# Second head of the first pair: hashed in 32x32 tiles, signs written in place, copies by ScalarE

## The chip, the cores and the metric

The kernel runs on one core of one Trainium2 chip. The metric is the time of one execution in device microseconds, as the median of several runs. A profiled execution gives the trace; its times are counted from the first instruction of the span.

## What is computed

Attention with a hash mask, then a mixture of small adapters. Four batches of eight heads, 768 positions, head size 64. The part that the change touches is the mask: a query and a key see each other only if the signs of their six projections agree.

```python
q_bits = (np.einsum('bhsd,dk->bhsk', q, proj) > 0)      # six bits a position
k_bits = (np.einsum('bhsd,dk->bhsk', k, proj) > 0)
...
mask = q_bucket[:, :, :, None] == k_bucket[:, :, None, :]
scores = scale * np.matmul(q, k.transpose(0, 1, 3, 2))
scores = np.where(mask, scores, -1000000000.0)
...
return np.matmul(attn, v).astype(np.float32)
```

Behind it, for each of the 3072 rows of the joined heads: the two best of eight experts by `x @ w_gate`, and their low-rank products added to `x`.

## The kernel before

The 32 heads are worked off as 16 pairs, `p` = 0 to 15. Each pair has six slots, `s` = 0 to 5. In a slot TensorE writes 128x1536 scores (`score`, L283), two blocks of 128 keys by 768 queries; slots 0 to 2 belong to the first head and 3 to 5 to the second. ScalarE takes the exponential of each (L286) into the tile `P`. Two PSUM buffers hold the scores, so the scores of a slot can be written while those of the slot before are being read. There are 96 slots. The order of everything is written out by hand: `slot` emits the scores and then the list `work(p)[s]`, and each engine runs its instructions in the order in which they are emitted.

The mask is worked into the score matmul. The operand tile `aug[p % 3]` has, for each of six blocks of 128 positions and for each of q and k of the two heads, 64 rows of the transposed head, six rows of signs (+0.5 or -0.5) and one row of a constant (1.0 for q, -1.5 for k). The contraction goes over these 71 rows; six equal signs add 1.5, which the constants take away, and any unequal sign leaves a negative number that the exponential, scaled by 128, sends to nothing.

How the rows get there, for pairs 1 to 15:

- `loadqk` (L152) and `loadv` (L160) fetch q, k and v from HBM on SyncE's queue, `natcast` (L232) makes bf16 of q and k on GpSimd, and `trq` (L241, TensorE) with `qcopy` (L247, VectorE), or a DMA transpose, puts them into `aug`. GpSimd's `shift` (L261) moves the second head's rows.
- `turn32` (L180) transposes 32x32 blocks of the same data on VectorE into `R`. `hash` (L193) multiplies `R` with the projection `hst` on TensorE, four groups of 32 output partitions (q and k of the two heads). `sign` (L205) compares with zero on VectorE into the tile `sg`.
- In `sg` the signs do not stand on the partitions where `aug` needs them. `signs_out` (L212) writes them to a DRAM tile `dr`, and `signs_in` (L220, or L224 for one head) reads them back into rows 64 to 71 of `aug`. The eight rows include the constant, which is made of `ssc`.

Pair 0 has a path of its own in `start`, because nothing else is there to hide its latencies. Its first head is transposed in fp32 by TensorE (`T1`, L540), copied out by ScalarE (`tcopy`, L544), cast into `aug` by ScalarE and GpSimd (`cast0`, L562), hashed from the transposed copy (`hash_here`, L568), and its signs are written straight into `aug` (`sign_here`, L575). Its second head is cast by GpSimd (`natcast0`, L548), transposed by TensorE (`tb0`, L553) and copied into `aug` by VectorE (`bcopy0`, L557), in slots 0 and 1; its signs take the way through `hash`, `sign` and DRAM, with `signs_out` on ScalarE's queue and `signs_in` on SyncE's queue in slot 0. `first(s)` emits what belongs to the first six slots. In `consts`, L90 writes the constant row of the first head with two memsets on VectorE.

The second product, of `P` with v, is `uni` (L291, one matmul that opens the sum) and `pvk` (L303, six matmuls for each block of keys), with `norm` (L321, L323) behind it. For pair 0 and its first head it stands in slots 4 and 5.

PSUM has two pools beside the two buffers of the scores: `m` with one buffer (hash, `trq`, router) and `vt` with one buffer (`tbB`, the transposes of pair 1's k, the sums of the second product).

Of the kernel before, what the change touches and what calls it, by code (L numbers as in the profile page):

```python
# [12 lines left out]
F32 = mybir.dt.float32  # L13
BF16 = mybir.dt.bfloat16
AX = mybir.AxisListType
ALU = mybir.AluOpType
# [3 lines left out]
class Emitter:  # L20
# [57 lines left out]
    def consts(self):  # L78
        nc, P, T, D, S = self.nc, self.P, self.T, self.D, self.S
        sg = self.singles  # L80
        self.wz = sg.tile([P, 512], BF16, name="wz")
        nc.vector.memset(self.wz, 0.0)
        self.dume = sg.tile([P, 1], F32, name="dume")
        nc.scalar.activation(out=self.dume, in_=self.wz[:, 0:1], func=ACT.Exp)
        self.ident = sg.tile([P, P], F32, name="ident")
        make_identity(nc, self.ident)
        self.aug = [sg.tile([P, T, 4, P], BF16, name=f"aug{i}") for i in range(3)]
        self.vb = [sg.tile([P, 2, T + 1, D + 1], BF16, name=f"vb{i}") for i in range(3)]
        for i in range(2):
            nc.vector.memset(self.aug[0][64:96, :, i, :], 1.0 if i == 0 else -1.5)  # L90
        self.eps = sg.tile([P, P], BF16, name="eps")
        nc.gpsimd.memset(self.eps, 2.0 ** -56)
        self.ident_bf = sg.tile([P, P], BF16, name="ident_bf")
        nc.gpsimd.tensor_copy(out=self.ident_bf, in_=self.ident)
        self.wa = sg.tile([P, self.nD, self.LZ], BF16, name="wa")
        self.Bcat = sg.tile([self.ER, self.Dm], BF16, name="Bcat")
        self.wg = sg.tile([P, self.nD, self.E], F32, name="wg")
        w = self.x3.tile([P, 2, self.Dm], F32, tag="acc", name="w")
        self.wA, self.wB = w[:, 0].rearrange("p (t z) -> p t z", t=self.nD), w[:, 1]
        for a in self.vb:  # L100
            nc.gpsimd.memset(a[:, :, 0:T, D:D + 1], 1.0)
            nc.gpsimd.memset(a[:, :, T:T + 1, D:D + 1], float(T))
        self.hst = sg.tile([P, 2, 8, 4], F32, name="hst")
        nc.gpsimd.memset(self.hst, 0.0)
        ssc = self.ssc = sg.tile([P, 1], F32, name="ssc")
        iq = sg.tile([P, 2], F32, name="iq")
        row = self.ident.rearrange("p (j b i) -> p j b i", j=4, b=8)
        nc.vector.memset(ssc, 0.5)
        for k in range(2):
            nc.vector.tensor_reduce(out=iq[:, k:k + 1], in_=row[:, k::2, 6, :], axis=AX.XY, op=ALU.add)  # L110
        for k, d in enumerate((-1.5, 1.0)):
            nc.vector.scalar_tensor_tensor(out=ssc, in0=iq[:, k:k + 1], scalar=d, in1=ssc,
                                           op0=ALU.mult, op1=ALU.add)
# [388 lines left out]
    def product(self, b, i, ps, start=True):  # L502
        self.nc.tensor.matmul(out=ps, lhsT=self.zT[b, i], rhs=self.Bcat, start=start, stop=True,  # L503
                              skip_group_check=not start)
# [38 lines left out]
    def tcopy(self, i):  # L543
        self.nc.scalar.mul(out=self.qkT[:, i, :], in_=self.tr["f", i][:, 0:384], mul=1.0 if i else 2.0 ** -10)  # L544

    def natcast0(self):
        for i in range(2):
            self.nc.gpsimd.tensor_copy(out=self.nb0[:, i], in_=self.nat[0][:, i, 1])  # L548

    def tb0(self, ps):  # L550
        for i in range(2):
            for u in range(3):
                self.nc.tensor.transpose(out=ps[:, i, u, :], in_=self.nb0[:, i, u * 128:(u + 1) * 128],  # L553
                                         identity=self.ident_bf)

    def bcopy0(self, e, ps):
        self.nc.vector.tensor_scalar(out=self.aug[0][0:64, e::2, 2:4, :].rearrange("p u i c -> p i u c"),  # L557
                                     in0=ps[64 * e:64 * e + 64], scalar1=2.0 ** -5, scalar2=None, op0=ALU.mult)

    def cast0(self, i, f):  # L560
        for e in range(2):
# [18 lines left out]
    def start(self):  # L580
        nc, P = self.nc, self.P
        sy, ac = nc.sync, nc.scalar
        self.proj3 = self.singles.tile([P, 32], F32, name="proj3")
        ac.dma_start(out=self.proj3[:, 0:6], in_=self.proj.unsqueeze(0).to_broadcast([2, 64, 6]))
        for h in range(2):
            for i in range(2):
                self.loadqk(0, i, h, sy)
        self.loadqk(1, 0, None, sy)
        self.loadqk(1, 1, None, sy)
        self.loadv(0, sy)  # L590
        self.loadqk(2, 0)
        self.loadqk(2, 1)
        nc.vector.memset(self.proj3[:, 6:32], 0.0)
        self.consts()
        self.qkT = self.singles.tile([P, 2, 384], F32, name="qkT")
        self.nb0 = self.singles.tile([P, 2, 384], BF16, name="nb0")
        w = [self.ps_s.tile([P, 3, 512], F32, tag="s", name="warm0")[:, 0], self.vt([P, 512], F32, "warm1")]
        warm = lambda n, i=1: self.warm(n, w[i])
        hq = self.ps_s.tile([P, 3, 512], F32, tag="s", name="hq")
        hk = self.ps_s.tile([P, 3, 512], F32, tag="s", name="hk")  # L600
        warm(5, 0)
        self.T1(0)
        self.T1(1, hk)
        warm(1)
        self.tcopy(0)
        self.tcopy(1)
        self.hst_fill(0, "dve")
        self.hst_fill(1, "pool")
        self.turn32(0, 0, 1)
        self.turn32(0, 1, 1)  # L610
        self.cast0(0, nc.scalar.copy)
        self.cast0(1, nc.gpsimd.tensor_copy)
        self.natcast0()
        self.hash_here(0, hq)
        self.hash_here(1, hk)
        self.hash(0, (1,))
        self.sign_here(0, hq, 0)
        self.sign_here(0, hq, 1)
        self.sign(0, (1,))
        self.signs_out(0, (1,), ac)  # L620
        for us in (slice(0, 1), slice(1, 3)):
            for e in range(2):
                self.sign_here(1, hk, e, us)

    def warm(self, n, w):
        for i in range(n):
            self.nc.tensor.matmul(out=w, lhsT=self.wz[:, 0:128], rhs=self.wz, start=True, stop=True)

    def first(self, s):
        if s == 0:  # L630
            tbB = self.tbB = self.vt([self.P, 2, 3, 128], BF16, "tbB")
            self.tb0(tbB)
            self.turn32(1, 0, 0)
            self.turn32(1, 1, 0)
            self.bcopy0(0, tbB)
            self.natcast(1, 0)
            self.natcast(1, 1)
            self.signs_in(0, (1,))
            self.loadv(1)
        if s == 1:  # L640
            self.hash(1, (0,))
            self.sign(1, (0,))
            self.signs_out(1, (0,))
            self.loadqk(3, 0)
            self.bcopy0(1, self.tbB)
            self.vcast(0)
        if s == 2:
            self.trq(1, 0)
            self.qcopy(1)
            self.trq(1, 1, self.vt)  # L650
            self.qcopy(1, 1)
            self.turn32(1, 0, 1)
            self.turn32(1, 1, 1)
            self.shift(1, 0)
            self.shift(1, 1)
            self.signs_in(1, (0,))
            self.loadqk(3, 1)
            self.natcast(2, 0)
            self.natcast(2, 1)
        if s == 3:  # L660
            self.hash(1, (1,))
            self.sign(1, (1,))
            self.signs_out(1, (1,))
            self.loadqk(4, 0)
            self.turn32(2, 0, 0)
            self.turn32(2, 0, 1)
            self.signs_in(1, (1,))
            self.vcast(1)
        if s == 4:
            self.turn32(2, 1, 0)  # L670
            self.turn32(2, 1, 1)
        if s == 5:
            self.trq(2)
            self.qcopy(2)
            self.shift(2, 0)
# [15 lines left out]
    def work(self, p):  # L691
# [3 lines left out]
        b, L, Ls, D = self.plan(p)  # L695
# [75 lines left out]
            add(4, "loadqk", n4, 1)  # L771

        if not last:
            kA = {4: (0, 1, 2), 5: (3, 4, 5)} if p == 0 else {4: (0, 1, 2, 3), 5: (4, 5)} if p == 1 or Ls == 3 else {
                3: (0, 1), 4: (2, 3), 5: (4, 5)}
            for s in sorted(kA):
                if s == min(kA):
                    add(s, "uni", p, 0)
                add(s, "pvk", p, 0, kA[s])
            add(5, "norm", p, 0)  # L780
# [7 lines left out]
        for s in sorted(D):  # L788
            d, i = D[s]
# [176 lines left out]
```

## Time and profile before

| | us |
|---|---|
| median of three runs | 167.91 |
| the three runs | 166.63, 167.91, 171.59 |
| the profiled execution | 167.42 |
| its span, first to last instruction | 165.6 |
| busy in the span: TensorE matmul | 149.5 |
| ScalarE | 143.6 |
| VectorE | 110.4 |
| GpSimd | 110.4 |

In the rows of the profile PE is TensorE, PEld its weight loads, DVE VectorE, ACT ScalarE, POOL GpSimd; SPq and ACTq are the queues of DMA issues of SyncE and ScalarE. A row of a timeline gives the start in us, the length in us, engine, line, instruction, output <- inputs, how many were merged, and in brackets the idle time before it with what ended it. A row of a group gives the busy time, the mean ns of one, and the idle time before. The ends of matmuls are modelled. One fp32 matmul appears as two records. The mean granted TensorE clock is 0.986.

### The profile page before, as it was taken

The page shows a single profiled execution, that of the slowest core. Times are in us where ns is not written, and L with a number is a line of the kernel's source. Part 1 is how long each engine was busy: PE and PEld are TensorE (multiplying, and loading weights), DVE is VectorE, ACT ScalarE, POOL GpSimd, SP SyncE. Part 2 cuts the span into 40 slices and gives each one's busy share as a digit, 9 for nine tenths or more (in the row PEclk, how much of TensorE's full clock was granted, in tenths as well). Part 3 has the DMA queues.
Part 4 walks back from the last instruction along what each step waited for, and adds up shares of the span by engine and source line. Part 5 has one row for each costly group of instructions (what it writes and reads, how often), then busy time and mean ns, then how long its engine had stood idle before and what let it go on. Part 6 is the DMA issues. An engine that isn't in the chain of part 4 may idle for free.

```text
span 165.6 us, 5300 instructions
## 1 busy us (share of the span) xinstructions
PE 149.5 (90%) x2148; PEld 101.8 (61%) x2148; DVE 110.4 (67%) x290; ACT 143.6 (87%) x122; POOL 110.4 (67%) x164
## 2 busy tenths in 40 slices
PE   6787998997999999999998999899999999999840
PEld 2244675675666666666765677576756666879500
DVE  5786895554747699486858696659766545656770
ACT  3466989798999999899998999989999999998640
POOL 3688969696878879694979397948976742510060
PEclk9999999999999999999999999999999999999995
DMA  5874659999999999999989999999998950439036
GB/s 146 279 246 117 199 125 205 260 237 224 169 202 190 211 190 241 185 214 340 256 178 254 321 255 155 251 247 285 174 245 153 248 94 4 86 124 294 6 132 248
DMA packets 58331, 33.09 MB, mean 200 GB/s; under 512 B 43714, under 2 KB 56002, under 8 KB 58306
## 3 DMA queue, kind: packets, MB, share of 16 engines
q1 hardware_dynamic: 57632, 32.46, 89.0%
q8 instruction: 17, 0.28, 0.7%
q10 hardware_dynamic: 674, 0.29, 0.6%
q14 instruction: 8, 0.07, 0.2%
HBM read 20.18 MB, written 7.05 MB: 164 GB/s over the span
## 4 chain that ended last, share of the span: by engine, by line
PE 49%; DMA 20%; DVE 16%; POOL 4%; issue 3%; SPq 3%; ACT 1%; DVEq 1%; POOLq 0%
PE s L283 21%; DMA nat<-in_k_dram 13%; PE pv L303 11%; DMA aug<-dr 5%; PE hs L193 4%; DVE R L180 3%; DVE acc L524 3%; PE pv L291 2%; DMA dr<-sg 2%; DVE x L323 2%; PE dl L503 2%; PE tr L241 2%; PE lz L405 2%; DVE gw L434 2%; DVE zm L436 1%
## 5 line engine op out<-in xcount | busy, mean ns | idle before, releaser
L286 ACT ACTIVATE P<-s 128x1536 bf16<-128x1536 f32 x96 | 135.3, 1450 | 11.3 <-PE s L283 9.0
L283 PE MATMUL s<-aug 71*128 71x512 bf16 (+2 forms) x432 | 78.5, 308 | 4.2 <-DMA aug<-dr 3.0
L283 PEld LDWEIGHTS <-aug 71*128 71x128 bf16 x432 | 34.2, 97 | 25.6 <-issue 8.0
L303 PEld LDWEIGHTS <-P 128*128 128x128 bf16 x1080 | 41.7, 98 | 7.2
L303 PE MATMUL pv<-vb,P 128*128 128x65 bf16 x1080 | 44.3, 193 | 0.0
L180 DVE STREAM_TRANSPOSE R<-nat 128x384 f32<-128x384 f32 x62 | 33.3, 560 | 5.8 <-DMA nat<-in_k_dram 4.9
L261 POOL COPY aug<-aug 64x768 bf16<-64x768 bf16 x30 | 24.8, 827 | 16.3 <-issue 11.1
L232 POOL CAST nb<-nat 128x768 bf16<-128x768 f32 x30 | 24.8, 828 | 2.0 <-DMA nat<-in_q_dram 0.7
L332 POOL CAST xb<-x 128x768 bf16<-128x768 f32 x15 | 12.4, 824 | 15.1 <-issue 6.5
L247 DVE TENSOR_SCALAR aug<-tr 128x768 bf16<-128x768 bf16 x20 | 11.0, 555 | 14.5 <-issue 6.5
L323 DVE TENSOR_TENSOR x<-pv,ri 128x384 f32<-128x384 f32 x30 | 16.7, 557 | 1.0
L170 POOL TENSOR_TENSOR vs<-vn 128x384 f32<-128x384 f32 x16 | 15.9, 996 | 0.0
L193 PE MATMUL hs<-R,hst 128*32 128x192 f32 x248 | 15.4, 332 | 0.2 <-DVE R L180 0.2
L524 DVE SCALAR_TENSOR_TENSOR acc<-dl,rt,x 128x512 f32<-128x512 f32 x18 | 13.3, 738 | 1.6 <-PE dl L503 1.6
L168 POOL CAST vb<-vn 128x768 bf16<-128x768 f32 x16 | 13.3, 828 | 0.2 <-DMA vn<-in_v_dram 0.2
L205 DVE TENSOR_SCALAR sg<-hs,ssc 128x192 bf16<-128x192 f32 (+1 forms) x17 | 7.1, 418 | 8.4 <-PE hs L193 8.4
L193 PEld LDWEIGHTS hs<-R,hst 128*32 128x32 f32 x248 | 7.2, 109 | 7.7 <-issue 2.5
L321 DVE RECIPROCAL ri<-pv 128x6 f32<-128x6 f32 x30 | 5.5, 184 | 9.4 <-PE pv L303 9.4
L291 PE MATMUL pv<-vb,eps 128*128 128x390 bf16 x30 | 10.1, 337 | 1.2 <-DVE x L323 0.6
L241 PE MATMUL tr<-ident_bf,nb 128*128 128x128 bf16 x120 | 10.0, 219 | 0.0
L241 PEld LDWEIGHTS <-nb 128*128 128x128 bf16 x120 | 8.4, 97 | 2.6
L522 POOL TENSOR_TENSOR acc<-acc,x 128x512 f32<-128x512 f32 x2 | 2.5, 1266 | 9.8 <-ACT acc L521 9.8
(111 smaller groups left out, 107.0 us busy)
## 6 DMA issues: line engine op xcount, KB each, us to landing
vn<-in_v_dram SPq DMA_DIRECT2D x16, 384.0 KB, 6.3
nat<-in_q_dram SPq DMA_DIRECT2D x15, 384.0 KB, 5.2
nat<-in_k_dram SPq DMA_DIRECT2D x15, 384.0 KB, 5.1
out_dram<-acc SPq DMA_DIRECT2D x7, 512.0 KB, 3.5
out_dram<-acc SPq DMA_DIRECT2D x9, 256.0 KB
dr<-sg SPq DMA_DIRECT2D x14, 48.0 KB, 5.0
aug<-dr SPq DMA_DIRECT2D x14, 48.0 KB
nat<-in_q_dram SPq DMA_DIRECT2D x2, 192.0 KB
```

Of the source, the lines that this page charges most:

```text
L170: nc.gpsimd.tensor_add(out=s3, in0=vn[:, :, 0:3, :], in1=vn[:, :, 3:6, :])
L180: self.nc.vector.transpose(out=self.R[p][:, i, h, :], in_=self.nat[p][:, i, h, :])
L193: nc.tensor.matmul(out=hs[32 * j:32 * j + 32], lhsT=self.hst[:, hf].rearrange("p b i -> p (b i)"), rhs=rhs, start=(hf == 0), stop=(hf == 1 ...
L232: self.nc.gpsimd.tensor_copy(out=self.nb[p][:, i].rearrange("p t h d -> p h t d"), in_=self.nat[p][:, i].rearrange("p h (t d) -> p h t d", ...
L241: self.nc.tensor.transpose(out=tr[:, t, :], in_=self.nb[p][:, i, t].rearrange("p h d -> p (h d)"), identity=self.ident_bf)
L261: self.nc.gpsimd.tensor_copy(out=a[0:64, :, 2 + i, :], in_=a[64:128, :, i, :])
L283: nc.tensor.matmul(out=ps[:, o:o + w].rearrange("p (t c) -> p t c", c=P), lhsT=aug[0:71, kt, 2 * h + 1, :], rhs=rhs, start=True, stop=True)
L286: nc.scalar.activation(out=self.P_[p][:, s * W:end], in_=ps, func=ACT.Exp, scale=128.0)
L291: self.nc.tensor.matmul(out=pv, lhsT=self.eps, rhs=self.vb[p % 3][:, h, T:T + 1, :].to_broadcast([self.P, T, D + 1]), start=True, stop=Fal ...
L303: self.nc.tensor.matmul(out=pv[:, i, :], lhsT=self.P_[p][:, o:o + P], rhs=vb[:, h, kt, :], start=False, stop=(kt == T - 1), skip_group_che ...
L323: nc.vector.tensor_tensor(out=self.x[b][:, :, c:c + D], in0=pv[:, :, 0:D], in1=ri.unsqueeze(2).to_broadcast([P, T, D]), op=ALU.mult)
L524: nc.vector.scalar_tensor_tensor(out=out, in0=ps, scalar=rt, in1=self.x[b][:, i, :], op0=ALU.mult, op1=ALU.add)
```

## The change

The second head of pair 0 no longer goes through DRAM for its signs.

- `hash1(i, ps)` multiplies each 32x32 block of `R` on its own, with eight columns of `hst`: rows 32n to 32n+31 of the array and output partitions 32n to 32n+7, n = 0 to 3, in two steps that accumulate. All of it lies in one PSUM tile `h1` of the pool `vt`.
- `sign1(i, ps)` compares on VectorE, four instructions of 6x192 for each of q and k, straight into `aug`.
- The casts, transposes and copies are split by q and k. The transposes (`tb0`) and copies move from slots 0 and 1 into `start`, and the copies (`bcopy0`) from VectorE to ScalarE, four instead of two. `tb` now lies in the pool `m`.
- In `start` the signs of the first head stand in another order among the 32x32 transposes, and the second head's k is transposed behind the first of them.
- The constant rows of the second head come from two memsets more, on GpSimd.
- In slots 3 and 4, `uni` and the first three key blocks of `pvk` move from slot 4 to slot 3, in front of the scores of slot 4; the hash of pair 1's second head, its sign, its way through DRAM, the load of pair 4's q and the cast of pair 1's v move from slot 3 to slot 4.

```diff
-        for i in range(2):
-            nc.vector.memset(self.aug[0][64:96, :, i, :], 1.0 if i == 0 else -1.5)
+        for i in range(4):
+            (nc.vector, nc.gpsimd)[i // 2].memset(self.aug[0][64:96, :, i, :], -1.5 if i % 2 else 1.0)
...
-    def bcopy0(self, e, ps):
-        self.nc.vector.tensor_scalar(out=self.aug[0][0:64, e::2, 2:4, :].rearrange("p u i c -> p i u c"),
-                                     in0=ps[64 * e:64 * e + 64], scalar1=2.0 ** -5, scalar2=None, op0=ALU.mult)
+    def bcopy0(self, i, ps):
+        for e in range(2):
+            self.nc.scalar.mul(out=self.aug[0][0:64, e::2, 2 + i, :], in_=ps[64 * e:64 * e + 64, i], mul=2.0 ** -5)
+
+    def hash1(self, i, ps):
+        for hf in range(2):
+            for n in range(4):
+                r = slice(32 * n, 32 * n + 32)
+                rhs = self.R[0][r, i, 1, :].rearrange("p (t f c) -> p f t c", f=2, c=32)[:, hf]
+                self.nc.tensor.matmul(out=ps[32 * n:32 * n + 8, i], lhsT=self.hst[r, hf, :, n], rhs=rhs,
+                                      start=(hf == 0), stop=(hf == 1), skip_group_check=True)
+
+    def sign1(self, i, ps, ts=slice(0, 6)):
+        for n in range(4):
+            self.nc.vector.tensor_scalar(
+                out=self.aug[0][64:70, ts, 2 + i, 32 * n:32 * n + 32], in0=ps[32 * n:32 * n + 6, i, ts],
+                scalar1=0.0, scalar2=0.5, op0=ALU.is_gt, op1=ALU.subtract)
...
         self.turn32(0, 0, 1)
-        self.turn32(0, 1, 1)
+        self.natcast0(0)
         self.cast0(0, nc.scalar.copy)
         self.cast0(1, nc.gpsimd.tensor_copy)
-        self.natcast0()
+        self.natcast0(1)
         self.hash_here(0, hq)
         self.hash_here(1, hk)
-        self.hash(0, (1,))
+        tb = self.m([P, 2, 3, 128], BF16, "tb")
+        h1 = self.h1 = self.vt([P, 2, 6, 32], F32, "h1")
         self.sign_here(0, hq, 0)
+        self.turn32(0, 1, 1)
+        self.tb0(0, tb)
+        self.hash1(0, h1)
+        self.tb0(1, tb)
+        self.bcopy0(0, tb)
+        self.bcopy0(1, tb)
         self.sign_here(0, hq, 1)
-        self.sign(0, (1,))
-        self.signs_out(0, (1,), ac)
...
         if s == 0:
-            tbB = self.tbB = self.vt([self.P, 2, 3, 128], BF16, "tbB")
-            self.tb0(tbB)
+            self.hash1(1, self.h1)
             self.turn32(1, 0, 0)
             self.turn32(1, 1, 0)
-            self.bcopy0(0, tbB)
+            self.sign1(0, self.h1)
             self.natcast(1, 0)
             self.natcast(1, 1)
-            self.signs_in(0, (1,))
             self.loadv(1)
         if s == 1:
             self.hash(1, (0,))
             self.sign(1, (0,))
             self.signs_out(1, (0,))
             self.loadqk(3, 0)
-            self.bcopy0(1, self.tbB)
+            self.sign1(1, self.h1)
             self.vcast(0)
...
         if s == 3:
+            self.uni(0, 0)
+            self.pvk(0, 0, (0, 1, 2))
+            self.turn32(2, 0, 0)
+            self.turn32(2, 0, 1)
+        if s == 4:
             self.hash(1, (1,))
             self.sign(1, (1,))
             self.signs_out(1, (1,))
             self.loadqk(4, 0)
-            self.turn32(2, 0, 0)
-            self.turn32(2, 0, 1)
             self.signs_in(1, (1,))
             self.vcast(1)
-        if s == 4:
             self.turn32(2, 1, 0)
             self.turn32(2, 1, 1)
```

`natcast0` and `tb0` take the argument `i` and do one of q and k, and `work` no longer emits `uni` and the first `pvk` for pair 0.

More of the change, by code (lines that the diff above doesn't have):

```diff
@@ L544, in tcopy, with natcast0, tb0 @@
         self.nc.scalar.mul(out=self.qkT[:, i, :], in_=self.tr["f", i][:, 0:384], mul=1.0 if i else 2.0 ** -10)
[L546 to L554, printed above, removed]
-    def bcopy0(self, e, ps):
-        self.nc.vector.tensor_scalar(out=self.aug[0][0:64, e::2, 2:4, :].rearrange("p u i c -> p i u c"),
-                                     in0=ps[64 * e:64 * e + 64], scalar1=2.0 ** -5, scalar2=None, op0=ALU.mult)
+    def natcast0(self, i):
+        self.nc.gpsimd.tensor_copy(out=self.nb0[:, i], in_=self.nat[0][:, i, 1])
+    def tb0(self, i, ps):
+        for u in range(3):
+            self.nc.tensor.transpose(out=ps[:, i, u, :], in_=self.nb0[:, i, u * 128:(u + 1) * 128],
+                                     identity=self.ident_bf)
+    def bcopy0(self, i, ps):
[13 more added lines that the diff above has]
+                scalar1=0.0, scalar2=0.5, op0=ALU.is_gt, op1=ALU.subtract)
     def cast0(self, i, f):
@@ L773, in work @@
         if not last:
[L774 removed]
+            kA = {5: (3, 4, 5)} if p == 0 else {4: (0, 1, 2, 3), 5: (4, 5)} if p == 1 or Ls == 3 else {
                 3: (0, 1), 4: (2, 3), 5: (4, 5)}
             for s in sorted(kA):
[L777 removed]
+                if s == min(kA) and p:
                     add(s, "uni", p, 0)
```

## The prediction

> **What bounds the kernel now.** I read the page first, then ScalarE's timeline, then the chain of waits, then the whole timeline of the first 40 us. In the page's list of the costliest groups the 96 exponentials of the scores stand first, and ScalarE's own timeline (start, length, instruction, idle time before it) shows how they follow each other:
>
> ```profile
> span 165.6 us, 5300 instructions
> L286 ACT ACTIVATE P<-s 128x1536 bf16<-128x1536 f32 x96 | 135.3, 1450 | 11.3 <-PE s L283 9.0
> 9.91 2.79 ACT L286 ACTIVATE P<-s 128x1536 bf16<-128x1536 f32 x2 [3.49 <-PE s L283]
> 12.89 1.45 ACT L286 ACTIVATE P<-s 128x1536 bf16<-128x1536 f32 x1 [0.19 <-PE s L283]
> 15.57 5.89 ACT L286 ACTIVATE P<-s 128x1536 bf16<-128x1536 f32 x4 [1.22 <-PE s L283]
> 21.72 7.63 ACT L286 ACTIVATE P<-s 128x1536 bf16<-128x1536 f32 x5 [0.26 <-PE s L283]
> 30.14 8.53 ACT L286 ACTIVATE P<-s 128x1536 bf16<-128x1536 f32 x6 [0.79 <-PE s L283]
> 39.36 22.69 ACT L286 ACTIVATE P<-s 128x1536 bf16<-128x1536 f32 x16 [0.69 <-PE s L283]
> ```
>
> The reader is to see that from 39.36 us on ScalarE hardly stops, so the end of the kernel is about the time at which it gets there plus a constant. Before that it loses 3.49 us ahead of the first exponential, then 0.19, 1.22, 0.26, 0.79 and 0.69. All these wait for score matmuls. The chain of waits (start, length, what) says what holds the fourth:
>
> ```profile
> 6.41 0.59 DVE R L180
> ...
> 8.19 0.42 DVE sg L205
> 8.64 4.05 DMA dr<-sg
> 12.71 0.35 SPq L224
> 13.11 1.55 DMA aug<-dr
> 14.71 0.82 PE s L283 x4
> ```
>
> The signs of the second head of pair 0 go out to DRAM and come back: 14.71 - 8.61 = 6.1 us. The same round trip blocks SyncE's queue, whose waits are listed apart, and in the timeline two later scores (pair 2 and pair 3, first step) wait for the same kind of transfer, issued late:
>
> ```profile
> SPq L224 <- DMA dr<-sg: 10.6, 3, 7.0
> 13.43 0.40 SPq L160 DMA_DIRECT2D vn<-in_v_dram  x1
> 13.93 0.69 SPq L212 DMA_DIRECT2D dr<-sg  x1
> 18.24 1.00 SPq L212 DMA_DIRECT2D dr<-sg  x1
> 22.70 0.38 SPq L212 DMA_DIRECT2D dr<-sg  x1
> 24.74 0.29 SPq L220 DMA_DIRECT2D aug<-dr  x1
> 29.22 0.82 PE L283 MATMUL s<-aug 71*128 71x512 bf16 x4 [0.99 <-DMA aug<-dr]
> 32.15 0.34 SPq L220 DMA_DIRECT2D aug<-dr  x1
> 38.44 0.82 PE L283 MATMUL s<-aug 71*128 71x512 bf16 x4 [1.03 <-DMA aug<-dr]
> ```
>
> **What goes.** The three small transfers go, and with them SyncE's 7.0 us wait, VectorE's two copies (L557) and one sign (L205) of this head, and four matmuls at L193. What they move is little; that other transfers stand behind them in SyncE's queue is what counts.
>
> **The signs, step by step.** These rows carry the costs on VectorE, TensorE, ScalarE and GpSimd (the rows of the groups give the mean of one in ns behind the busy time):
>
> ```profile
> L575 DVE TENSOR_SCALAR aug<-hq 6x384 bf16<-6x384 f32 x2 | 1.1, 558 | 0.0
> L575 DVE TENSOR_SCALAR aug<-hk 6x128 bf16<-6x128 f32 x2 | 0.6, 283 | 0.1
> 5.12 0.83 PE L568 MATMUL hq<-qkT,proj 64*32 64x384 f32 x4
> 8.64 1.50 DVE L575 TENSOR_SCALAR aug<-hk 6x128 bf16<-6x128 f32 x4
> 10.17 1.04 DVE L180 STREAM_TRANSPOSE R<-nat 128x384 f32<-128x384 f32 x2
> L544 ACT ACTIVATE qkT<-tf 128x384 f32<-128x384 f32 x1 | 0.5, 492 | 0.7 <-PE tf L540 0.7
> 15.46 0.84 PE L193 MATMUL hs<-R,hst 128*32 128x192 f32 x8
> 19.90 0.86 PE L193 MATMUL hs<-R,hst 128*32 128x192 f32 x16
> 9.02 0.85 PE L283 MATMUL s<-aug 71*128 71x512 bf16 x4 [1.14 <-issue]
> 9.71 0.50 PE L553 MATMUL tbB<-ident_bf,nb 128*128 128x128 bf16 x6
> 4.33 0.88 POOL L117 COPY hst<-proj 32x6 f32<-32x6 f32 x4 [2.33 <-DMA proj<-in_proj_dram]
> 5.63 1.07 POOL L562 CAST aug<-qkT 64x384 bf16<-64x384 f32 x2 [0.42 <-ACT qkT L544]
> L548 POOL CAST nb<-nat 128x384 bf16<-128x384 f32 x2 | 1.0, 506 | 0.1
> L90 DVE MEMSET aug<- 32x768 bf16 x2 | 1.4, 698 | 0.3 <-issue 0.2
> 17.07 0.71 PE L303 MATMUL pv<-vb,P 128*128 128x65 bf16 x18
> ```
>
> VectorE: the first sign of the first head's q needs the hash matmuls that end at 5.12 + 0.83 = 5.95 us; it now stands ahead of the transpose of k, in what is idle time (the data of k come just before 6.41). So 6.0 to 6.55, then the transpose (0.59) to 7.15, the second sign to 7.7, and the four signs of k (1.50) from 7.7 to 9.2, where they ended at 10.14: 0.9 us earlier. The two transposes of pair 1 (1.04) go to 10.3.
>
> TensorE and GpSimd: GpSimd casts the second head's q at 5.25 to 5.75, does its half of the first head (1.07) to 6.8, and casts k to 7.3. TensorE transposes q (half of 0.50) and hashes q before that, transposes k by 7.75, and begins the first scores when the first sign of k is there, at 7.7 + 0.28 + 0.1 = 8.1; they end at 9.0.
>
> ScalarE: the wait ahead of the four copies is for the second transpose, so 7.8 + 4 x 0.49 = 9.75 us. A PSUM copy of 384 elements is the nearest row. The first exponential starts at 9.8 instead of 9.91: the 3.49 us of idle time cover the copies almost to the last tenth. Three exponentials then end at about 14.05.
>
> The second head: the eight hash matmuls of q, or of k, are sixteen records at four places of the array; the row with sixteen records at four column places took 0.86 us, the one with eight at two places 0.84. I take 0.85 for each half. The second half follows the first scores, 8.95 to 9.8; second scores to 10.5, pair 1's hash to 11.35. For a sign of 6x192 the rows of 128 and 384 elements (283 and 558 ns) give 0.35 us between them; the sign that goes, L205 in the chain, took 0.42 for as many elements. So the first four run 10.3 to 11.7, pair 1's sign to 12.15, the last four to 13.55 (by 0.42: 14.1). The transpose of pair 1's k writes the same PSUM buffer as this hash, so it waits for the last sign: 13.6 to 13.95. Fourth scores 14.0 to 14.85, fourth exponential at 14.9 against 15.57: 0.67 us gained, 0.1 by the dearer sign. Between these I take 0.5, near the cheap end because L575 has the same form (six partitions, immediate scalars), less something for three more changes of the matmul's shape. ScalarE still idles there about 1 us: VectorE is late in place of the transfer.
>
> GpSimd's two added memsets cost 1.4 us by VectorE's row and lie in 2.33 us of idle time before 4.33; were they over 2.3 us, all of the start would move by the excess. The new order of slots 3 and 4 puts one matmul of L291 and the 18 of L303 (0.71) in front of the fifth scores where pair 1's second hash stood (0.84), and needs nothing that is not there: nil, and its cover is the exponential before it (22.69 / 16 = 1.42). It makes pair 1's second hash a slot (1.5 us) later, and so its round trip, which SyncE issued at 18.24; by the times above the sign would be ready at 17.7, so nothing is late, but the margin is gone if VectorE falls behind.
>
> **The queue.** SyncE now passes from the loads of pair 2 straight to V of pair 1, at 12.7 - 7.0 = 5.7 us instead of 13.43, into the time up to 20 us. The table of windows shows the DMA engines half busy from 10 to 20:
>
> ```profile
> 10.00:20.00 10.00, 8.98 (x103) 5.36 (x104) 8.23 (x18) 8.42 (x6) 8.75 (x13) 1.00 0.54 159
> ```
>
> The last two figures are DMA share and GB/s. Pair 1's signs go out at 12.2 and not at 13.93; the loads behind move up by 1 to 2 us, and pair 2's signs, issued at 22.70 behind the return of pair 1's, can go 1 to 2 us earlier. Their return (issued 24.74, landed by 29.2) comes as much earlier, the score that needs it 0.5: most of the 0.79 us wait at 30.14 goes, I take 0.7. Pair 3's transfer stands behind a full queue (32.15 to 38.4) and should move as the work does, so its 0.69 us stays.
>
> The sum: 0.5 + 0.7 = 1.2 us off 167.42 us, the profiled execution's time (1.8 us around its span): **166.2 us**. The median of the three runs shown is 167.91, 0.5 above; about 2% is what a measurement of this kernel can tell from no change, so this is inside it.
>
> **Rivals.** *The gain is used up by the next wait.* The transfers of pairs 2 and 3 land when the DMA engines allow, and ScalarE meets them anyway at 30.14 and 39.36: 167.2 us, 0 to 0.4 gained. For it: pair 3's transfer takes 38.4 - 32.15 = 6.25 us, which no edit touches. Against it: less is left to load by then.
>
> *The row tiles do not run together.* The four 32x32 matmuls of a step read different rows of the array and write one PSUM bank. The trace has no such case: at L568, where two row halves run at once, each has a bank of its own. If they run one after the other, sixteen records at 0.84 / 4 = 0.21 us make 3.4 us and not 0.85. The first half then ends near 10.0, the copies at 12.2, the second half at 14.6, and the fourth exponential starts near 18.6: 3.0 us late. Some of it is met again at 30.14 (0.79 us of wait), so plus 2.2 to 3.0, about 170 us. The change is slower than before from the point at which a half takes over 1.4 us, where the gain of 1.2 is spent on both halves.
>
> The Trainium skill, "TensorEngine Tiling (Array Packing)", section "Restrictions and Gotchas", says that different row tiles cannot write the same PSUM bank at the same time and that software must keep them apart. By that rule, if the array itself held them apart, this rival's time would be the result. Another page, "PSUM — Partial Sum Buffer", section on bank collisions, tells of errors only where such tiles share the same 32 partitions too, which these don't. No run here shows either yet.
>
> *Both later waits go.* With the whole 0.67, and 0.26, 0.79 and 0.69 on top: 165.0 us. ScalarE's further gaps come after 60 us and are not the start's; only if loads that run ahead shrink them too does it go under 2%.
>
> **How the numbers follow.** Forecast 0.48, its own range 165.5 to 166.9; gain used up 0.18; row tiles in turn 0.16; both waits gone 0.18. The range 164.7 to 170.0 leaves out half of each of the last two, 0.17 together, and takes in both prices of a sign. Over 2% faster (under 164.1): 0.10, the part of the last rival in which the later gaps shrink as well. Over 2% slower (over 170.8): 0.11, row tiles in turn with the dear sign on top, and with pair 1's signs late for their margin is then gone. Within 2%: 0.79.
>
> **What would show it.** The fourth exponential at 14.9 to 15.4 us with VectorE's sign as the last releaser; sixteen records of the new hash within 0.9 us; no idle time before the first scores of pair 2; SyncE's transfer of V for pair 1 before 7 us. Wrong if the new hash takes over 1.4 us a half, if the first exponential is later than 9.91, or if the gain at the fourth is gone by 39.36.

## The result, and the profile after

| | us |
|---|---|
| changed kernel, median of 20 runs | 168.38 (166.81 to 170.32) |
| kernel before, median of 20 runs | 167.45 (165.05 to 171.69) |
| ratio, 95% interval | 1.0101 (1.0063 to 1.0140) |
| profiled execution of the changed kernel, and its span | 166.81, 165.0 |

The kernel became about 1% slower. It is within 2%, but the interval lies above 1; the forecast was 1.2 us less. The ratios in this text compare only executions within 1.5% of their kernel's fastest (here fifteen of the changed kernel and ten of before), so they are not the ratio of the medians. The profiled execution is the shortest of the twenty, so the trace is read for its places and not for its total.

In this execution the start came as forecast; the repeated runs below show how much of that stands. First ScalarE's own timeline of the changed kernel (start, length, instruction, idle time before it):

```profile
7.98 2.00 ACT L556 ACTIVATE aug<-tb 64x384 bf16<-64x384 bf16 x4 [1.63 <-PE tb L551]
10.00 4.14 ACT L286 ACTIVATE P<-s 128x1536 bf16<-128x1536 f32 x3
14.98 6.07 ACT L286 ACTIVATE P<-s 128x1536 bf16<-128x1536 f32 x4 [0.84 <-PE s L283]
21.31 38.77 ACT L286 ACTIVATE P<-s 128x1536 bf16<-128x1536 f32 x27 [0.26 <-PE s L283]
60.10 0.23 ACT L426 ACTIVATE e<-d 128x24 f32<-128x24 f32 x1
```

The fourth exponential starts at 14.98 us, and from 21.31 us 27 follow without a break: the waits that stood at 30.14 and 39.36 are gone. The same kernel's whole timeline shows the new work (here L556 is `bcopy0`, L563 `hash1`, L568 `sign1`, and L587, further down, `sign_here`):

```profile
1.36 1.41 POOL L90 MEMSET aug<- 32x768 bf16 x2
5.36 0.96 SPq L160 DMA_DIRECT2D vn<-in_v_dram  x1
6.52 0.84 PE L563 MATMUL h<-R,hst 32*8 32x192 f32 x16
8.85 0.84 PE L563 MATMUL h<-R,hst 32*8 32x192 f32 x16
10.36 1.46 DVE L568 TENSOR_SCALAR aug<-h 6x192 bf16<-6x192 f32 x4
12.28 1.46 DVE L568 TENSOR_SCALAR aug<-h 6x192 bf16<-6x192 f32 x4
13.80 0.49 PE L241 MATMUL tr<-ident_bf,nb 128*128 128x128 bf16 x6 [0.99 <-DVE aug L568]
```

In these two executions the gain is lost between 60 and 130 us. The exponential at L426 (the router's first) stands at 62.07 us in before and at 60.10 here, but the spans are 165.6 and 165.0 us: of 1.97 us, 0.6 is left. ScalarE's timeline of before behind that point, then of the changed kernel:

```profile
62.07 0.22 ACT L426 ACTIVATE e<-d 128x24 f32<-128x24 f32 x1
66.78 13.08 ACT L286 ACTIVATE P<-s 128x1536 bf16<-128x1536 f32 x9 [0.46 <-PE s L283]
90.27 7.33 ACT L286 ACTIVATE P<-s 128x1536 bf16<-128x1536 f32 x5 [0.54 <-PE s L283]
108.08 7.33 ACT L286 ACTIVATE P<-s 128x1536 bf16<-128x1536 f32 x5 [0.60 <-PE s L283]
```

```profile
64.80 5.60 ACT L286 ACTIVATE P<-s 128x1536 bf16<-128x1536 f32 x4 [0.46 <-PE s L283]
70.66 7.33 ACT L286 ACTIVATE P<-s 128x1536 bf16<-128x1536 f32 x5 [0.25 <-PE s L283]
88.46 7.33 ACT L286 ACTIVATE P<-s 128x1536 bf16<-128x1536 f32 x5 [0.59 <-PE s L283]
106.95 7.33 ACT L286 ACTIVATE P<-s 128x1536 bf16<-128x1536 f32 x5 [1.27 <-PE s L283]
124.61 7.33 ACT L286 ACTIVATE P<-s 128x1536 bf16<-128x1536 f32 x5 [0.45 <-PE s L283]
```

Three waits of 1.60 us together have become five of 3.02. The first of each list (0.46 us) ends before the first load of the chain below has landed; the others, two of 1.14 us together, have become four of 2.56. The chain of waits of the changed kernel shows what these stand behind (start, length, what):

```profile
62.58 0.37 SPq L489
62.95 0.05 issue
63.01 4.84 DMA nat<-in_k_dram
67.84 0.02 issue
67.87 1.04 DVE R L180 x2
68.91 0.64 DVE acc L524
69.55 0.04 issue
69.59 0.38 PE dl L503
69.97 0.22 PE s L283
...
80.91 4.74 DMA nat<-in_k_dram
...
98.72 5.42 DMA nat<-in_k_dram
...
117.58 4.21 DMA nat<-in_k_dram
```

Read it from the end: the scores wait behind a matmul of the router (L503), which waits for VectorE to free its PSUM buffer (L524), which stands in VectorE's queue behind the 32x32 transposes of the next pair's k (L180). These wait for the load of k, and that load is issued by SyncE behind the router's DMA transpose at L489. Once in every two pairs this load sets the pace, four times in all. The same rows in the chain of before:

```profile
65.33 4.38 DMA nat<-in_k_dram
...
83.44 4.02 DMA nat<-in_k_dram
...
100.78 4.50 DMA nat<-in_k_dram
...
118.44 4.06 DMA nat<-in_k_dram
```

From issue to landing the load takes 4.24 us in the mean of four before, 4.80 after, at the same place of a program that is unchanged there. No edit touches it.

### The profile page after: what moved, and what is told of

It reads as the page before. It is cut to its first block, busy times and chain, and to the rows that moved or that the text cites. A ratio compares the mean times of both kernels' runs of the same rounds, so it can differ in the third digit from the quotient of the medians.

```text
span 165.0 us, 5351 instructions
## 1 busy us (share of the span) xinstructions
PE 150.2 (91%) x2171; PEld 101.8 (62%) x2172; DVE 111.4 (67%) x295; ACT 145.5 (88%) x126; POOL 111.7 (68%) x166
## 4 chain that ended last, share of the span: by engine, by line
PE 56%; DVE 21%; DMA 14%; issue 3%; ACT 1%; SPq 1%; DVEq 1%
PE s L283 23%; PE pv L303 13%; DMA nat<-in_k_dram 12%; PE hs L193 5%; DVE R L180 4%; PE tr L241 3%; PE pv L291 3%; DVE x L323 3%; DVE acc L524 3%; PE dl L503 2%; DMA nat<-in_q_dram 2%; PE lz L405 2%; DVE gw L434 2%; DVE aug L568 2%; DVE aug L587 1%
## 5 line engine op out<-in xcount | busy, mean ns | idle before, releaser
L180 DVE STREAM_TRANSPOSE R<-nat 128x384 f32<-128x384 f32 x62 | 33.1, 559 | 4.9 <-DMA nat<-in_k_dram 4.1
L524 DVE SCALAR_TENSOR_TENSOR acc<-dl,rt,x 128x512 f32<-128x512 f32 x18 | 13.3, 739 | 1.6 <-PE dl L503 1.6
L193 PE MATMUL hs<-R,hst 128*32 128x192 f32 x240 | 13.7, 332 | 0.0
L193 PEld LDWEIGHTS hs<-R,hst 128*32 128x32 f32 x240 | 6.6, 109 | 6.2 <-DVE ri L321 2.5
L503 PE MATMUL dl<-Bcat,zT 128*128 128x512 bf16 x18 | 6.8, 378 | 3.0 <-DVE acc L524 3.0
```

The lines of the kernel that those rows point to most:

```text
L180: self.nc.vector.transpose(out=self.R[p][:, i, h, :], in_=self.nat[p][:, i, h, :])
L193: nc.tensor.matmul(out=hs[32 * j:32 * j + 32], lhsT=self.hst[:, hf].rearrange("p b i -> p (b i)"), rhs=rhs, start=(hf == 0), stop=(hf == 1 ...
L524: nc.vector.scalar_tensor_tensor(out=out, in0=ps, scalar=rt, in1=self.x[b][:, i, :], op0=ALU.mult, op1=ALU.add)
```

## The experiments

**Both kernels again, and the load moved.** `b_again` and `a_again` are the two kernels as they are. `c_load` (on before) and `d_load` (on the changed kernel) have only the load taken out of its place behind L489. `zt_dma` is the transpose at L489, which waits for VectorE; `gates` and `gsum` are VectorE's work around it:

```diff
+            if p == 1:
+                add(4, "loadqk", 5, 0)
+            add(4, "loadqk", n4, 1)
             if L:
                 for f in ("gates", "zt_dma", "gsum"):
                     add(Ls + 1, f, b, L)
-            if p == 1:
-                add(4, "loadqk", 5, 0)
-            add(4, "loadqk", n4, 1)
```

> The kernel before, unchanged, for a second trace and the spread of the comparison. Both theories: ratio 1.00. In its trace the start should repeat (fourth exponential near 15.6 us, waits of 0.8 and 0.7 us ahead of 30.1 and 39.4), and the waits between 60 and 130 us for the loads of k should come to 1.6 us within 0.8 either way if they are a matter of how long a load happens to take.

> The changed kernel, unchanged, for a second trace. Theory A (the start gains about 1.9 us by 60 us as in the first trace, and the waits for the loads of k between 60 and 130 us take it back): the exponential numbered 18 starts near 37.4 us again, and ScalarE's gaps after 60 us are larger than in the kernel before by 1 us or more. Theory B (the start itself varies and its gain is not there in most runs): the exponential numbered 18 starts after 38.5 us. Ratio 1.00 to 1.01 in both.

> The kernel before with one move: the load of k for the pair four ahead is issued by SyncE ahead of the transpose of the gated product (L489), not behind it. Theory A: SyncE waits for VectorE at L489, the load behind it lands some 4 to 5 us after that, and VectorE, TensorE and ScalarE wait in turn; with the load about 1.9 us earlier the gaps at pairs 6, 8, 10 and 12 go and the kernel gains 1.0 to 2.0 us, ratio 0.988 to 0.994. Theory B: these waits come from the rate of the DMA engines and the order of issue changes nothing, ratio 0.997 to 1.003.

> The changed kernel with the same move. Theory A: the gain of the start is no longer taken back, so it comes on top of the move: 1.0 to 1.9 us under the kernel before with the move, ratio to the kernel before 0.978 to 0.985. Theory B: no better than the kernel before with the move, ratio 0.99 to 1.01.

Measured: `b_again` 1.0013 (0.9967 to 1.0059), `a_again` 1.0107 (1.0064 to 1.0150), `c_load` 0.9875 (0.9816 to 0.9935), `d_load` 0.9879 (0.9821 to 0.9938). So the slowdown repeats, and it hangs on this load: taken from behind L489 it lets both kernels run 1.2% under the time before, and nothing is left of the difference between them. For `d_load` that is a miss of theory A, which expected the start's gain on top of the move. ScalarE's waits for scores between 60 and 130 us come to 1.29 us in `b_again` and to 5.62 in `a_again`.

The repeats also show that the start's gain mostly isn't there. The fourth exponential of `b_again`, then that of `a_again`:

```profile
14.94 1.45 ACT L286 ACTIVATE P<-s 128x1536 bf16<-128x1536 f32 x1 [0.54 <-PE s L283]
```

```profile
15.45 6.06 ACT L286 ACTIVATE P<-s 128x1536 bf16<-128x1536 f32 x4 [1.45 <-PE s L283]
```

With no edit at all, before gets there at 14.94 us, because its signs take 3.33 us to DRAM and not 4.05 (its chain of waits), and the changed kernel gets there at 15.45. VectorE's timeline of the changed kernel in its first trace, then in `a_again`, says why the latter is late:

```profile
5.97 0.56 DVE L587 TENSOR_SCALAR aug<-hq 6x384 bf16<-6x384 f32 x1
6.56 0.58 DVE L180 STREAM_TRANSPOSE R<-nat 128x384 f32<-128x384 f32 x1
```

```profile
6.43 0.56 DVE L587 TENSOR_SCALAR aug<-hq 6x384 bf16<-6x384 f32 x1 [1.09 <-PE hq L580]
7.02 0.58 DVE L180 STREAM_TRANSPOSE R<-nat 128x384 f32<-128x384 f32 x1
```

The first sign of q now stands ahead of the transpose of the second head's k. In `a_again`, `d_load` and `d_load2` the sign waits for its hash until 6.35 to 6.54 us, and the transpose behind it starts at 6.93 to 7.13, where it starts at 6.3 to 6.5 in before, `b_again` and `c_load`. In all four traces of the new start the fourth exponential comes 8.4 us behind that transpose. Its mean is 15.34 us in these four and 15.38 in the three of the old start.

`b_again` also has no wait at 30 or 39 us (27 exponentials in a row from 21.60 us), with its L426 at 60.63 us: those two waits come and go with the execution. Why the load takes longer in the changed kernel was still open.

**What falls into the load.** Besides the kernel's own transfers, the page's list of DMA queues has two for instructions, q14 with 8 packets and q8 with 17. Of the changed kernel, the row of q8 for the whole run, and then the same row asked for the time from issue to landing of each of the four loads (packets, MB, share of 16 engines' time):

```profile
q8 instruction: 17, 0.28, 0.8%
...
q8 instruction: 1, 0.02, 1.4%
...
q8 instruction: 1, 0.02, 1.2%
...
q8 instruction: 1, 0.02, 1.5%
...
q8 instruction: 1, 0.02, 2.2%
```

Seventeen packets of 16 KB in the run, and one in each of the four loads. The same four questions to before are answered without such a row. The packets are code, and TensorE's by their count, as the rows of busy time of before and of the changed kernel show (busy us, share, number):

```profile
PE 149.5 (90%) x2148; PEld 101.8 (61%) x2148; DVE 110.4 (67%) x290; ACT 143.6 (87%) x122; POOL 110.4 (67%) x164
```

```profile
PE 150.2 (91%) x2171; PEld 101.8 (62%) x2172; DVE 111.4 (67%) x295; ACT 145.5 (88%) x126; POOL 111.7 (68%) x166
```

2171 + 2172 records in 17 packets are 255 a packet; no other engine has nearly so many, and `k_after_split` below, with 208 instructions more on TensorE, has an eighteenth packet. The Trainium skill, "Runtime: NRT & Kernel Launch", section "Instruction fetch mechanics", says that an engine's instructions are refilled in blocks of 16 KiB, 256 instructions, through a DMA queue that the sequencer drives, and that crossing a block is mostly hidden. Size and count agree with these rows. Whether it is hidden is what the next runs ask.

Between the issue of two such loads the changed kernel's table of windows counts TensorE's records (length, then busy time and number of records of TensorE's matmuls, its weight loads, VectorE, ScalarE and GpSimd, then granted clock, DMA share and GB/s):

```profile
63.01:80.91 17.90, 17.37 (x258) 12.01 (x259) 12.90 (x34) 17.00 (x14) 13.51 (x19) 1.00 1.03 238
```

258 matmuls and 259 weight loads, two blocks to within a few instructions. So where a block falls against the load is nearly the same all four times, and it is decided by how many instructions TensorE has had before. The change adds 47 records (4343 against 4296), nearly all at L563: 32 fp32 records with their weight loads in place of eight.

**TensorE's instructions alone.** `f_before_pe48` is before with 48 instructions more; the warm-up matmuls on zeros, ahead of all work, are cut into five:

```diff
-        for i in range(n):
-            self.nc.tensor.matmul(out=w, lhsT=self.wz[:, 0:128], rhs=self.wz, start=True, stop=True)
+        for c in [slice(512 * j // 5, 512 * (j + 1) // 5) for j in range(5)] * n:
+            self.nc.tensor.matmul(out=w[:, c], lhsT=self.wz[:, 0:128], rhs=self.wz[:, c], start=True, stop=True)
```

> Before, with each of the six warm-up matmuls (512 columns) cut into five narrower ones: 24 matmuls and 24 weight loads more on TensorE, 48 instructions, about as many as the change adds there (twelve fp32 matmuls at four each, less three waits, 45); nothing else is changed. Theory F (the time of code): TensorE's instructions come in blocks of 16 KB, 17 of them in a run (the row of the instruction queue), one every 8.8 us, which is half of the 17.6 us between two of the loads of k that stand behind L489; so a block falls at the same place of each such load. In the two traces of before it starts 4.2 to 6.9 us behind the issue of that load, when the load has landed (4.25 us); in the two of the changed kernel 0.9 to 3.2 us behind it, inside the load, which then takes 4.85. 48 instructions should move it there here too: load 4.7 to 5.0 us, blocks 1 to 3.5 us behind its issue, more idle time of ScalarE between 65 and 130 us, and with none of the change's gain at the start 1.008 to 1.016 of the time before. Theory R (the turn in which transfers take their eight semaphores, moved by three) and theory S (the order of slots 3 and 4, or the earlier queue of SyncE) leave this kernel as it was: 0.996 to 1.004, load 4.25.

Measured: 1.0128 (1.0056 to 1.0200). The chain of waits of this run, then its row of the instruction queue over each of the four loads:

```profile
67.04 5.41 DMA nat<-in_k_dram
...
85.52 4.66 DMA nat<-in_k_dram
...
103.50 4.62 DMA nat<-in_k_dram
...
121.19 5.01 DMA nat<-in_k_dram
```

```profile
q8 instruction: 1, 0.02, 1.2%
...
q8 instruction: 1, 0.02, 1.5%
...
q8 instruction: 1, 0.02, 2.1%
...
q8 instruction: 1, 0.02, 1.2%
```

Nothing of the change is in this kernel, its DMAs and their order are those of before, and its first and fourth exponentials start at 9.88 and 15.62 us (before 9.91 and 15.57). Yet the blocks lie in the loads, these take 4.93 us in the mean, and the loss is there. Theory S is not needed for the loss, for this kernel has neither the new order of slots nor the earlier queue; `i_after_less48` and `k_after_split` below have both and do not lose. TensorE is idle for 0.53 of the 17.90 us in the row of windows above, which holds two blocks, so the trace agrees with that section of the Trainium skill as far as TensorE goes: there the block is nearly hidden. The load that it meets is not spared.

`e_after_dma3` gives every transfer the semaphore that it had in before, with three small transfers in slot 0 in place of the three that the change takes out:

```diff
             self.natcast(1, 1)
+            for i in range(3):
+                dum = self.singles.tile([1, 6], F32, name=f"dum{i}")
+                self.nc.sync.dma_start(out=dum, in_=self.proj[0:1, :])
             self.loadv(1)
```

> The changed kernel, with three transfers of 24 bytes on SyncE's queue in slot 0, in place of the three that the change takes out: from there on every transfer has the semaphore that it had before. Theory R: the loads behind L489 land in 4.25 us again, 0.984 to 0.996 of the time before. Theories F and S: as the changed kernel, 1.006 to 1.014, loads 4.8 to 5.0.

Measured: 1.0174 (1.0111 to 1.0238), and loads of 4.65 to 5.95 us. Theory R falls. Time and loads lie above what theory F expected too, and why is open.

**Moving the blocks out again.** `g_after_pe108` and `h_load_pe108` use the same edit as `f_before_pe48` with ten cuts instead of five, on the changed kernel and on `d_load`. `i_after_less48` takes as many instructions out of the changed kernel as the change puts in, by leaving work out. `k_after_split` computes everything and goes the other way round, by nearly a whole block. The edit of `i_after_less48`, then that of `k_after_split`:

```diff
-            self.pvk(0, 0, (0, 1, 2))
+            self.pvk(0, 0, (0,))
...
-            kA = {5: (3, 4, 5)} if p == 0 else
+            kA = {5: (5,)} if p == 0 else
```

```diff
+            if 6 * p + s < 26:
+                for f in (0, w // 2):
+                    nc.tensor.matmul(out=ps[:, o + f:o + f + w // 2].rearrange("p (t c) -> p t c", c=P),
+                                     lhsT=aug[0:71, kt, 2 * h + 1, :],
+                                     rhs=rhs[:, f // P:(f + w // 2) // P], start=True, stop=True)
+                at += w
+                continue
             nc.tensor.matmul(out=ps[:, o:o + w].rearrange("p (t c) -> p t c", c=P), lhsT=aug[0:71, kt, 2 * h + 1, :],
                              rhs=rhs, start=True, stop=True)
```

> The changed kernel, with each warm-up matmul cut into ten: 108 instructions more on TensorE ahead of all else, which should move the blocks of code 4 to 6.5 us earlier against the work, to 2 to 4 us ahead of the issue of the loads behind L489 and so out of them. Theory F: those loads 4.1 to 4.4 us, the start's gain stays, 0.984 to 0.994 of the time before, unless the block meets the transpose that is issued 1.2 us ahead of the load. Theories R and S: as the changed kernel, 1.006 to 1.014, loads 4.8 to 5.0.

> The changed kernel with the load moved ahead of the transpose at L489 (as in the run d_load) and the warm-up matmuls cut into ten. In d_load a block of code started 3.6 to 4.2 us behind that load and 3 us behind the transpose, which then took 5.5 us twice. Theory F: blocks 4 to 6.5 us earlier, transposes at L489 under 4.3 us, 0.975 to 0.985. Theories R and S: as d_load, 0.982 to 0.994.

> The changed kernel without four of the six key blocks of pair 0's first head in the product with v: 24 matmuls and 24 weight loads less on TensorE (48 instructions), 1 us of TensorE's time before 20 us, where ScalarE sets the pace. Theory F, which the run of before with 48 instructions more has borne out: blocks of code come as late as in before (3.9 to 4.2 us ahead of the loads behind L489 and 4.2 to 6.9 behind their issue), loads 4.1 to 4.4 us, and with the start's gain 0.984 to 0.995 of the time before. Against it: something else of the change slows those loads, then 4.8 to 5.0 us and 1.006 to 1.014.

> The changed kernel, nothing left out, with every score matmul of the first 26 slots cut in two: 104 matmuls and 104 weight loads more, 208 instructions, which with the change's own 45 is nearly one block of 256, so that the blocks stand against the work as in before. Theory F: loads behind L489 4.1 to 4.5 us. The cuts cost TensorE 0.1 to 0.2 us a slot of its slack: 0.986 to 1.002 of the time before, with less idle time of ScalarE between 65 and 130 us than in the changed kernel. Against it: 1.006 to 1.02, loads 4.8 to 5.0.

This table is worked out from the traces' packet and landing records: TensorE's instructions against before (of the program, where the 47 records go with three waits less), and for each of the four loads behind L489, where the nearest 16 KB packet starts (us behind the issue of the load; one that starts at or after the landing does not touch it), the time to landing, its mean, and the measured ratio to before.

```
                instr.   packet starts         load lands after         mean   ratio
before             0     6.0  4.2  4.6  5.1    4.38 4.02 4.50 4.06      4.24
b_again            0     6.8  4.3  5.7  4.4    4.42 4.13 4.48 4.03      4.27   1.0013
i_after_less48    -3     5.8  4.3  4.4  4.1    4.32 3.23 4.40 3.94      3.97   0.9877
k_after_split   +253     6.4  4.3  6.2  4.1    4.44 4.19 4.67 3.93      4.31   0.9887
g_after_pe108   +153     0.4 -1.6 -0.5 -2.1    5.00 4.13 4.95 3.97      4.51   1.0109
after            +45     2.9  2.5  3.2  1.1    4.84 4.74 5.42 4.21      4.80   1.0101
a_again          +45     1.3  2.5  1.0  2.3    4.96 4.98 5.13 4.64      4.93   1.0107
f_before_pe48    +48     3.4  2.2  1.2  3.1    5.41 4.66 4.62 5.01      4.93   1.0128
e_after_dma3     +45     2.8  3.1  3.4  3.3    4.65 5.21 5.95 5.39      5.30   1.0174
```

The profiled executions are single ones, some of them among the longer of their kernel, so loads and packets are compared here, and the verdicts go by the ratios. A long execution as such does not make the loads long: `k_after_split` was profiled in the second longest of its eight (169.12 us), the changed kernel in its shortest.

The rest of the span behind the first L426 (L433 in `k_after_split`) goes the same way. Where the granted clock is 1.00 from 60 to 130 us, it is 102.7 to 103.6 us in the first four rows and 104.5 to 105.2 in `g_after_pe108`, the changed kernel and `f_before_pe48`. At a clock of 0.98 and 0.95, `a_again` and `e_after_dma3` take 107.6 and 108.9.

`i_after_less48` 0.9877 (0.9784 to 0.9970, from three of its six executions) and `k_after_split` 0.9887 (0.9806 to 0.9969, from four of eight): with fewer instructions, and with many more, the packets start about where they did in before, the loads land in 4.0 and 4.3 us, and the changed kernel is faster than before. That it works from both sides rules out that TensorE's added work as such costs the time.

`g_after_pe108` was a miss: 1.0109 (1.0068 to 1.0149). The blocks moved by 3.4 us and not by 4 to 6.5, and now fall at the edge of the load or on the transpose in front of it; two loads of four still take 5 us. Its first exponential is late too, at 10.53 us, but with the same cuts `h_load_pe108` has it at 9.87, so that is not shown to be the cuts' doing. It tells nothing against the theory and little for it.

`h_load_pe108` missed its number too: 0.9892 (0.9829 to 0.9956) where 0.975 to 0.985 was expected (three of six executions), and the transposes at L489 took 4.64 to 5.49 us, not under 4.3. Its blocks came 1.4 to 2.1 us behind the moved load, in the middle of it, and the load takes 4.84 us in the mean, yet the time is that of `d_load`. Once the load has been issued ahead of L489, a block in it does no harm that can be measured.

**The two kernels with the load moved, once more.**

> Before with the load ahead of the transpose at L489, as in the run c_load, again beside the next one: 0.984 to 0.992. Its blocks of code start 2.1 to 2.9 us ahead of the load and 5.5 to 6.7 behind its issue.

> The changed kernel with the load ahead of the transpose at L489, as in the run d_load, again beside c_load2. Theory F: its blocks fall 3.6 to 4.2 us behind the load, on the transposes behind it, which have slack, so the start's gain is kept in part: 0.980 to 0.990, at or up to 1 us under c_load2. Against it: equal or over c_load2.

Measured: `c_load2` 0.9877 (0.9829 to 0.9924), `d_load2` 0.9853 (0.9778 to 0.9928). Both beat the two kernels of this study. Between them nothing is settled: medians 165.79 and 165.31 us here, 165.90 and 164.45 in the first pair of runs, with six runs of each `d_load`; the ratios differ by less than their intervals.

## Why the prediction was wrong

The time lies in the range and the new work costs about what was forecast, but the gain at the start came in one trace of four, and the kernel became slower. By the prediction's own steps:

- **First exponential at 9.8 us.** 10.00. The copies took 2.00 us, from 7.98; forecast were 4 x 0.49 from 7.8. By the prediction's own sign, later than 9.91, this is a miss, of a tenth of a us; in `a_again`, `d_load` and `d_load2` it is 9.77 to 9.97.
- **Hash halves at 0.85 us.** 0.84 each. The rival of row tiles that run in turn, at 3.4 us a half, is out. The Trainium skill, "TensorEngine Tiling (Array Packing)", section "Restrictions and Gotchas", has the rule that different row tiles cannot write one PSUM bank at the same time; the trace does not bear it out for these four tiles, each of which writes other partitions of the bank.
- **Signs at 0.35 us.** 1.46 / 4 = 0.365. The transpose of pair 1's k waits for the last of them, as said.
- **0.5 us at the fourth exponential.** In the first trace 0.59 came, 14.98 for 15.57, and that was luck: over the traces it is 15.34 against 15.38. The step that failed here is the first sign of q ahead of the transpose of k, "in what is idle time". It went by one hash that ended at 5.95 us. In three of four traces the hash ends some 0.4 to 0.5 us later, and the sign holds the transpose up.
- **GpSimd's two memsets hidden.** 1.41 us from 1.36, hidden.
- **SyncE's queue.** V of pair 1 goes out at 5.36 us (5.7). The wait of pair 2's scores is gone, and pair 3's too, which was to stay. But `b_again` lacks both without any edit, so the 0.7 us was a term read off one execution. L426 comes at 62.07, 60.63 and 60.90 us in before, `b_again` and `c_load`, and at 60.10, 60.57, 60.67 and 60.48 us in the changed kernel, `a_again`, `d_load` and `d_load2`: 0.7 us between the means, where 1.2 was forecast, and most of it is the 62.07 of one trace.
- **The step that made the sign wrong** is in the first part: that ScalarE hardly stops from 39.36 us on, so that "the end of the kernel is about the time at which it gets there plus a constant". It is no constant: the rest of the span behind L426 is 103.5 and 102.9 us in before and `b_again`, 104.9 and 105.2 in the changed kernel and `f_before_pe48`. The gaps "after 60 us" that were set aside as "not the start's" are mostly waits for four loads of k, and the change moves TensorE's blocks of code into them. `f_before_pe48` puts a price on moving the blocks alone, wherever they fall: 1.28% of 167.42 us, 2.1 us (0.9 to 3.3), where the whole forecast gain was 1.2.
- **The rival of a gain used up by the next wait** was nearest, but it named the transfers of pairs 2 and 3, at 30.14 and 39.36, and ended at no worse than no change. The wait that took the gain is another one, and it takes more than the gain.
- **The rival of a slower kernel**, row tiles in turn, was the wrong one: it looked for the loss in the new matmuls' time. The loss came from their number.

What the change is worth without the collision is not settled. `i_after_less48` and `k_after_split` say about 1.2%, from few executions and with intervals that reach from 0.3 to 2.2%, and the former leaves work out. With the load moved, the two kernels do not differ (0.9875 and 0.9879, 0.9877 and 0.9853), and the start shows little. So the forecast of 0.7% is neither confirmed nor ruled out for the kernel as the prediction thought of it. That the block delays the load on the way that the landing records suggest (next section) is argued; that moving TensorE's instruction count alone moves the blocks, the loads and the time is shown.

## What to carry to other kernels

In a program with a repeating stage, ask where the blocks of code of the busiest engine fall against the transfers that the stage waits for; if the period is close to a whole number of blocks, every edit to that engine's instruction count ahead of it, however small, shifts all later stages alike. A load that sets the pace has to be issued early enough to bear that: here, one load moved ahead of the transfer in front of it took 1.2% off, and a block that fell into it there cost nothing that could be measured. An instruction put into another's idle time in front of it is free only while its own input comes early enough. And a wait seen in one execution is a term of a sum only if a second execution has it too.

## What the runs showed of the hardware

- A 16 KB packet of code takes 0.9 to 1.7 us between 60 and 130 us (packet records of before, `b_again`, the changed kernel and `f_before_pe48`), and the load that it meets at L489 lands late by its last parts, not as a whole. Each load lands in 16 parts; in the mean of the four loads the median part lands 3.56 us behind the issue in before, 3.52 in the changed kernel and 3.47 in `f_before_pe48`, the last part 0.68, 1.28 and 1.46 us later. In the changed kernel one to seven of the sixteen parts come in that late group. Which DMA engines carry the packet and the late parts, these traces do not say.
- The blocks do not move in step with the count: 45 instructions moved them by about 2.6 us (from a mean of 5.0 us behind the issue to 2.4), and 108 more by 3.4 us, in traces where TensorE runs some 29 instructions in a us (517 in 17.90 us).
- Four row tiles of 32x8 that write one PSUM bank ran at once: 16 records in 0.84 us, each of them 0.32 to 0.33 us long by the trace, with four starting within 0.02 us and the next four 0.16 to 0.17 us later.
